# GpSimd's routed and output transfers wait for matmuls at chosen places instead of for copies of their row numbers

## The chip, the cores and the metric

The kernel runs on one core of a Trainium2 chip. The metric is the device time of one execution in microseconds (us), the median of three runs. TensorE (PE in the profile) multiplies matrices, VectorE (DVE), ScalarE (ACT) and GpSimd (POOL) work on rows, and SyncE (SP) issues most of the plain transfers. GpSimd issues the indirect ones, whose destination rows come from a column of row numbers in on-chip memory.

## The reference, cut to what matters

A long convolution of 8 sequences of 5056 steps and 128 channels is followed by a mixture of experts with 4 groups of 4 experts. Every token goes to the best expert of its best group.

```python
# x: [8, 5056, 128], h: [5056, 128]
L = 2 * S
y = np.fft.irfft(np.fft.rfft(x, n=L, axis=1) * np.fft.rfft(h, n=L, axis=0)[None], n=L, axis=1)[:, :S, :]
x = y.reshape(40448, 128)
g_logits = x @ w_group                       # 4 groups
g_idx, g_w = argmax, softmax weight of it
for g in range(4):
    e_logits = xg @ w_expert[g]              # 4 experts of the group
    e_idx, e_w = argmax, softmax weight of it
    for e in range(4):
        h = np.maximum(xg[mask_e] @ w1[g, e], 0.0)   # 128 -> 1024
        out[tok_idx] = g_w * e_w * (h @ w2[g, e])    # 1024 -> 128
```

## The kernel before, in words

The convolution is done as Fourier transforms written as matmuls, in three rounds r = 0, 1, 2 of at most three sequences. A round has a first stage (`stage1`, matmuls of L427 and L433, whose results ScalarE and VectorE copy and combine in L444 to L450) and then `groups`: a forward transform (L531), the multiplication by the transform of h on VectorE (L549), an addition (L583), an inverse transform (L599) and a copy `zs` on ScalarE (L612) that is stored to memory.

Beside the main list of each later round runs a `side` list with the tokens of the round before: the last inverse transform (L734 to L748, copied to `yT` in L755), transposes (L791) into rows `rw` (L792), the logits (L802 to L812), and the gate on VectorE (`gate_math`, L910 to L1003), which ends in `posf` (L1003): for each token the row of the array `srt` in which it is to lie, so that tokens of one expert lie together. Then `srt` receives the rows: for each 128 tokens one closure of `scatter` (L863) stands in the list `sends`. `send()` takes the next closure. It copies one column of `posf` to the integers `pos` (L867), on VectorE or on ScalarE as the caller asks, and lets GpSimd issue the indirect transfer of L868 out of `rw`. Calls of `send` stand at fixed places of the main list.

The experts are then worked off in blocks of 512 tokens, each in 8 steps. A step has three matmuls of the first layer (`mm1`, L1374 to L1376, into `px` or `aux`), the ReLU on ScalarE (L1379) and the rest of its split on VectorE (L1380), and three matmuls of the second layer (`mm2`, L1392 to L1394, into `pz` or `ptr`). ScalarE copies the result (`oT`, L1397), TensorE turns it (L1408), VectorE scales it (`orow`, L1412), and `scatter_out` lets GpSimd issue one indirect transfer to `out` for each 128 rows (L1445). In the blocks that have a fixed place in the program (`timed`) ScalarE first copies the column of row numbers, `ids` or `kept_ids`, to a tile `at` of which there are 8 (L1443). Some blocks of rows go out to memory and come back later as `take`. From about 1485 us the last blocks run, whose transfers use `sids` and no copy.

The order of every engine's instructions is that of the program; nothing reorders it. `run` writes the main list, and `weave` puts the side lists between its steps by weights. A transfer that GpSimd issues waits, before the change, for the engine that wrote its column of row numbers. Thus the place of the copy on ScalarE or VectorE sets when a transfer starts.

Of the kernel before, what the change touches and what calls it, by code (L numbers as in the profile page):

```python
# [232 lines left out]
class Kernel:  # L233
# [5 lines left out]
    def pools(self, ctx):  # L239
# [5 lines left out]
        self.turns, self.beside, self.sends, self.tick = 0, "", [], 0  # L245
# [136 lines left out]
    def stage1(self, r):  # L382
# [32 lines left out]
        def mm(k):  # L415
# [7 lines left out]
            for j in range(h * QB // 2, (h + 1) * QB // 2):  # L423
                if fold:
                    for b in range(2):
                        for c in range(2):
                            nc.tensor.matmul(  # L427
# [4 lines left out]
                else:  # L432
                    nc.tensor.matmul(  # L433
# [37 lines left out]
    def groups(self, r):  # L471
# [42 lines left out]
        def forward(p):  # L514
# [7 lines left out]
            for i, (to, of, w) in enumerate(steps):  # L522
                for b in range(2):
                    rows = slice(b * 64, b * 64 + 64)
                    for c in range(2):
# [5 lines left out]
                        nc.tensor.matmul(  # L531
                            px[c * 64:c * 64 + 64, b, to], lhsT=k, rhs=data[:, of],
                            start=begin, stop=i == len(steps) - 1 or p == 0 and i == 1, tile_position=(b * 64, c * 64),
                        )
            if r == 0:
# [21 lines left out]
        def product(p):  # L557
# [9 lines left out]
            self.send("a")  # L567
# [8 lines left out]
            if r == 2 and p % 2 == 0 and len(self.sends) > 12:  # L576
                self.send("a")
# [9 lines left out]
        def inverse(p):  # L587
# [7 lines left out]
            for part in range(2):  # L595
                wt, k = (cgs[p + LP], 320 - part * 64) if p > 0 else (first[0], part * 128)
                for c in range(n):
                    for h in (0, 64):
                        nc.tensor.matmul(  # L599
# [46 lines left out]
        def step(k):  # L646
# [4 lines left out]
            self.tick += 1  # L651
# [47 lines left out]
    def side(self, r):  # L699
# [39 lines left out]
        def rest(n):  # L739

            zt = zts.pop(n // 4)
            for u in range(nu):
                for q in (n // QB, n // QB + 1):
                    k = q % 2 * QB * RT
                    for c in (0, 64):
                        d = c * nu + u * HD
                        both = pys[q][c:c + 64, 0:QB * c1].rearrange("p (i u m) -> p i u m", i=QB, u=nu)[:, :, u]
                        nc.tensor.matmul(  # L748
# [4 lines left out]
            for q in (n // QB, n // QB + 1):  # L753
                k = QB * q % 8 * c1
                nc.scalar.copy(out=self.yT[:, k:k + QB * c1], in_=pys.pop(q)[:, 0:QB * c1])  # L755

        def lump(k):
            def f():
# [8 lines left out]
                rest(4 * k)  # L767

# [9 lines left out]
        def rows(i):  # L778
# [10 lines left out]
            for j in range(n):  # L789
                k = (4 * i + j) * GP  # L790
                nc.tensor.transpose(out=pt[:, j * D:(j + 1) * D], in_=self.yT[:, k:k + GP], identity=self.ident)  # L791
# [38 lines left out]
        for o in range(N2 // 8):  # L830
# [3 lines left out]
            if r < 2:  # L834
# [3 lines left out]
                at.append((t + 4.7, both(lm, lambda: rows(0)), False))  # L838
                at.append((t + 6.4, both(lt, lambda: rows(1)), False))
                at.append((t + 9.5, both(*more), False))  # L840
                at += [(t + 6.5 + 5.6 * k / (NMATH + REST), advance(ops), True) for k in range(NMATH + REST)]
                at.append((t + 12.15, lambda o=o, s=sends: self.sends.extend((8 * r + o, f, self.tick) for f in s), True))
            else:
# [4 lines left out]
                at.append((t + 3, both(lm, lambda: rows(0)), False))  # L848
                at.append((t + 4, both(lt, lambda: rows(1)), False))
                at.append((t + 5, both(*more), False))  # L850
                at += [(t + 4.02 + 3.3 * k / (NMATH + REST2), advance(ops), True) for k in range(NMATH + REST2)]
                at.append((t + 7.4, lambda o=o, s=sends: self.sends.extend((8 * r + o, f, self.tick) for f in s), True))
# [10 lines left out]
    def scatter(self, k, j, p, r, T):  # L863


        def f(copy):
# [920 lines left out]
```

## Time and profile before

| | before |
|---|---|
| median of 3 runs (lowest, highest) | 1764.83 us (1753.78, 1769.3) |
| the profiled execution, its span | 1761.84 us, 1760.3 us |
| mean granted clock of TensorE | 0.989 |
| TensorE busy | 1649.6 us, 94% |
| VectorE busy | 1317.5 us, 75% |
| ScalarE busy | 1118.5 us, 64% |
| GpSimd busy | 763.5 us, 43% |

The span is the profiled execution from its first to its last recorded instruction. Busy time counts an engine's own instructions, without register and semaphore work. Four stretches of the span bear on the change: rounds 1 and 2 with their side lists (192 to 700 us), the expert blocks beside which the last tokens are routed (700 to 1116 us), the expert blocks with output transfers at fixed places (1116 to 1485 us), and the last blocks (1485 to 1760 us). In the rows below, "idle" is an engine's time without work just ahead of an instruction, and the name behind the arrow is what ended it. "issue" means that the engine waited for nothing that the profile shows.

### The profile page before, as it was taken

What the parts mean: (1) busy time and instruction counts of PE and PEld (TensorE: products, weight loads), DVE (VectorE), ACT (ScalarE), POOL (GpSimd) and SP (SyncE); (2) the same over time, 40 slices, a digit from 0 to 9 for tenths busy, and PEclk for the clock granted to TensorE, in tenths of its full rate; (3) what the DMA queues carried; (4) which work ended last, traced back from release to release, by engine and by line L of the source; (5) the groups of instructions that cost most, each with busy time, mean ns of one, the idle gap of its engine ahead of it and who ended that gap; (6) DMA issues with size and microseconds to landing.
All of it is one profiled execution on the core that took longest, in us unless ns stands there. A gap on an engine that the chain in (4) does not pass through costs nothing. (4 is left out here: it accounts for less than half of the span.)

```text
span 1760.3 us, 47512 instructions
## 1 busy us (share of the span) xinstructions
PE 1649.6 (94%) x16576; PEld 1267.6 (72%) x16576; DVE 1317.5 (75%) x2969; ACT 1118.5 (64%) x2645; POOL 763.5 (43%) x730
## 2 busy tenths in 40 slices
PE   8998898988889898999999999999999999999998
PEld 7676745546755554777777777787777877888987
DVE  6554587864567677687787778888788888887888
ACT  5554444443444444677777777677777777776876
POOL 1451232333244445325455545345555555334545
PEclk9999999998999999999999999999999999999999
DMA  7797576766666787676666755476965687555667
GB/s 212 225 289 214 161 230 215 254 204 201 176 199 212 232 242 214 176 187 178 166 177 165 176 151 142 115 177 185 213 171 138 167 216 199 141 135 147 165 159 176
DMA packets 403939, 330.22 MB, mean 188 GB/s; under 512 B 167708, under 2 KB 347425, under 8 KB 403672
## 3 DMA queue, kind: packets, MB, share of 16 engines
q1 hardware_dynamic: 374808, 271.01, 56.9%
q0 software_dynamic: 20608, 41.79, 7.3%
q10 hardware_dynamic: 8256, 14.10, 2.8%
q8 instruction: 139, 2.28, 0.6%
q14 instruction: 128, 1.05, 0.2%
HBM read 208.00 MB, written 96.86 MB: 173 GB/s over the span
## 5 line engine op out<-in xcount | busy, mean ns | idle before, releaser
L868 POOL DMA_INDIRECT srt<-rw,pos x320 | 334.0, 1044 | 491.1 <-ACT pos L867 141.0
L1445 POOL DMA_INDIRECT out<-orow,at x176 | 190.8, 1084 | 237.1 <-ACT at L1443 122.9
L549 DVE TENSOR_TENSOR y<-pp,hg 128x768 f32<-128x768 f32 (+1 forms) x108 | 92.5, 857 | 93.9 <-ACT hg L539 33.4
L1445 POOL DMA_INDIRECT out<-orow,sids x92 | 96.2, 1045 | 114.8 <-DVE orow L1412 89.3
L599 PE MATMUL pp<-y,cg 64*64 64x384 f32 (+1 forms) x1504 | 132.0, 444 | 13.2 <-issue 6.5
L531 PE MATMUL pp<-st,cg 64*64 64x192 f32 (+1 forms) x1588 | 121.5, 404 | 4.0 <-issue 1.9
L755 ACT COPY yT<-py 128x474 f32<-128x474 f32 (+1 forms) x96 | 44.7, 513 | 116.8 <-PE py L748 88.5
L612 ACT COPY zs<-pp 128x768 f32<-128x768 f32 (+1 forms) x106 | 75.6, 714 | 64.5 <-PE pp L599 38.2
L445 DVE TENSOR_TENSOR st<-pp,odd 128x320 f32<-128x320 f32 x96 | 46.9, 489 | 91.4 <-ACT odd L444 87.4
L734 PE MATMUL py<-ig,zm 126*64 126x79 f32 x2048 | 92.3, 237 | 21.6 <-issue 18.8
L734 PEld LDWEIGHTS py<-ig,zm 126*64 126x64 f32 x2048 | 78.9, 137 | 43.1 <-issue 35.1
L599 PEld LDWEIGHTS pp<-y,cg 64*64 64x64 f32 x1504 | 62.4, 132 | 61.5 <-issue 40.2
L1380 DVE SCALAR_TENSOR_TENSOR h3l<-px,h3h 128x512 fp32r<-128x512 f32 (+1 forms) x111 | 74.4, 671 | 40.9 <-ACT h3h L1379 39.1
L1380 DVE SCALAR_TENSOR_TENSOR h0l<-px,h0h 128x512 fp32r<-128x512 f32 (+1 forms) x109 | 73.3, 672 | 37.2 <-ACT h0h L1379 26.5
L531 PEld LDWEIGHTS pp<-st,cg 64*64 64x64 f32 x1588 | 66.5, 133 | 43.5 <-issue 29.6
L1379 ACT ACTIVATE h0h<-px 128x512 fp32r<-128x512 f32 (+1 forms) x109 | 64.0, 587 | 50.8 <-PE px L1376 38.0
L1380 DVE SCALAR_TENSOR_TENSOR h2l<-px,h2h 128x512 fp32r<-128x512 f32 (+1 forms) x112 | 75.3, 672 | 23.8 <-ACT h2h L1379 15.3
L549 DVE TENSOR_TENSOR m<-pp,hg 128x768 f32<-128x768 f32 (+1 forms) x108 | 91.5, 847 | 0.0
L792 ACT COPY rw<-py 128x1024 uint16<-128x1024 uint16 (+1 forms) x88 | 81.1, 938 | 16.1 <-remote 6.8
L1379 ACT ACTIVATE h3h<-px 128x512 fp32r<-128x512 f32 (+1 forms) x111 | 65.3, 589 | 32.4 <-PE px L1376 20.9
L583 POOL TENSOR_TENSOR y<-y,m 128x512 f32<-128x512 f32 x40 | 50.9, 1277 | 77.3 <-DMA hd<-hg 43.0
L1380 DVE SCALAR_TENSOR_TENSOR h1l<-px,h1h 128x512 fp32r<-128x512 f32 (+1 forms) x111 | 74.4, 671 | 11.3 <-issue 7.7
(482 smaller groups left out, 5248.3 us busy)
## 6 DMA issues: line engine op xcount, KB each, us to landing
wr<-in_moe_w SPq DMA_DIRECT2D x373, 256.0 KB
zd<-zs SPq DMA_DIRECT2D x66, 384.0 KB
zm<-zd SPq DMA_DIRECT2D x64, 378.0 KB
cg<-in_c_g SPq DMA_DIRECT2D x106, 224.0 KB
zd<-zs SPq DMA_DIRECT2D x39, 256.0 KB
hg<-hd SPq DMA_DIRECT2D x68, 128.0 KB
xt<-in_x ACTq DMA_DIRECT2D x52, 160.0 KB
zm<-zd SPq DMA_DIRECT2D x32, 252.0 KB
```

What stands on the lines that cost most here:

```text
L445: nc.vector.tensor_tensor(out=all_st[:, 0:2 * HALF, d], in0=even, in1=odd, op=ALU.add)
L531: nc.tensor.matmul(px[c * 64:c * 64 + 64, b, to], lhsT=k, rhs=data[:, of], start=begin, stop=i == len(steps) - 1 or p == 0 and i == 1, til ...
L549: nc.vector.tensor_tensor(out=t[:, :, 0:w].rearrange("p t (r u d) -> p t r u d", r=2, u=nu), in0=taken(px, part).unsqueeze(1).broadcast_to ...
L583: (nc.gpsimd if r == 0 else nc.vector).tensor_tensor(out=y[:, :, 0:w], in0=y[:, :, 0:w], in1=m[:, :, 0:w], op=ALU.add)
L599: nc.tensor.matmul(pz[c][h:h + 64, 0:w], lhsT=wt[c * 64:c * 64 + 64, k + h:k + h + 64], rhs=y[c * 64:c * 64 + 64, part, 0:w], start=part = ...
L612: nc.scalar.copy(out=z[:, 0:n, 0:w], in_=pp[:, 0:n, 0:w])
L734: nc.tensor.matmul(pys[q][c:c + 64, col(n, u)], lhsT=zms[q][:, n % QB, k:k + 64], rhs=self.ig[:, 0:NH], start=n % QB == 0 and u == 0, stop ...
L792: nc.scalar.copy(out=od["rw"][i // 2][:, 4 * i % RH:4 * i % RH + n, 0:2 * D].rearrange("p j (h d) -> p j h d", h=2), in_=pt[:, 0:n * D].bi ...
L868: ins = self.nc.gpsimd.indirect_dma_start(out=self.srt, out_offset=bass.IndirectOffsetOnAxis(ap=k["pos"][0:p, j:j + 1], axis=0), in_=k["rw ...
L1379: nc.scalar.activation(out=hh, in_=p, func=AF.Relu)
L1380: nc.vector.scalar_tensor_tensor(out=hl, in0=p, scalar=0.0, in1=hh.bitcast(F32), op0=ALU.max, op1=ALU.subtract)
L1445: ins = self.nc.gpsimd.indirect_dma_start(out=self.a["out"], out_offset=bass.IndirectOffsetOnAxis(ap=ids, axis=0), in_=o, in_offset=None, ...
```

## The change

The copies of L867 and L1443 are gone. The gate's last multiplication writes the integers `pos` itself, and output transfers read `ids` or `kept_ids` itself. In their place the program keeps in `self.mark` the latest matmul of certain kinds, and a new function `behind` makes a transfer wait for the one that is in `mark` when the transfer is written into the program. Marks are set in the first stage, in the forward and inverse transforms, in the side lists' matmuls and transposes, and at the last matmul of each `mm1` and each `mm2`. The calls of `send` have partly other places: fewer in the first stage and in the transforms, new ones in the side lists (`beside`) while these run next to a round, and at every step of the first expert blocks.

```diff
@@ stage1, groups, side: marks @@
-                    nc.tensor.matmul(
+                    self.mark = nc.tensor.matmul(
                         whole[:, j * 256:j * 256 + N1], lhsT=views[i][:, j * 128:j * 128 + 128], rhs=self.f,
...
+                if i == 1 and p % 2 == 0:
+                    self.mark = last
...
-                        nc.tensor.matmul(
+                        last = nc.tensor.matmul(
                             px[c * 64:c * 64 + 64, b, to], lhsT=k, rhs=data[:, of],
...
+            if p % 2 == 1:
+                self.mark = last
...
@@ groups: places of send @@
-            self.send("a")
+            self.send()
             yield
             m = multiply(px, p, 1, "m", 2)
...
-            if r == 2 and p % 2 == 0 and len(self.sends) > 12:
-                self.send("a")
...
-                    if p == k:
-                        self.send("a")
...
-                    if r == 2 or i == 1:
-                        self.send("s")
+                    if i == 1 or len(self.sends) > 20:
+                        self.send()
@@ side @@
+        def beside():
+            if self.beside != "experts":
+                self.send()
...
-                at.append((t + 4.7, both(lm, lambda: rows(0)), False))
+                at.append((t + 4.7, both(lm, lambda: rows(0), beside), False))
@@ scatter, send, behind @@
-        def f(copy):
-            copy(out=k["pos"][:, j:j + 1], in_=k["posf"][:, j:j + 1])
+        def f():
             ins = self.nc.gpsimd.indirect_dma_start(
                 out=self.srt,
...
+            self.behind(ins)
...
-    def send(self, eng="v"):
-
-        if eng == "a":
-            eng = "s" if self.sends and self.sends[0][2] < self.tick else "v"
+    def send(self):
+
         if self.sends:
-            self.sends.pop(0)[1](self.nc.vector.tensor_copy if eng == "v" else self.nc.scalar.copy)
+            self.sends.pop(0)[1]()
+
+    def behind(self, ins):
+
+        if self.mark is not None:
+            info = mybir.DependencyInfo(mybir.DependencyClass.Sync, mybir.DependencyReason.DATA)
+            self.tc.add_manual_dep(ins.ins, self.mark.ins.name, info, reason="transfers are issued one by one")
@@ gate_math @@
-        posf = tl([], "posf", bufs=2)
+        posf = tl([], "posf")
...
-        nc.vector.tensor_tensor(out=posf, in0=posf, in1=sg, op=ALU.mult)
-        k["posf"] = posf
         k["pos"] = cx.tile([128, 15], I32, name="pos", bufs=3)[0:P, 0:T]
+        nc.vector.tensor_tensor(out=k["pos"], in0=posf, in1=sg, op=ALU.mult)
@@ mm1, mm2 @@
-            nc.tensor.matmul(o, lhsT=wh[:, k:k + 128], rhs=xl, start=False, stop=True)
+            self.mark = nc.tensor.matmul(o, lhsT=wh[:, k:k + 128], rhs=xl, start=False, stop=True)
...
-            nc.tensor.matmul(p, lhsT=wh[:, k:k + 128], rhs=hl, start=False, stop=f == 7)
+            self.mark = nc.tensor.matmul(p, lhsT=wh[:, k:k + 128], rhs=hl, start=False, stop=f == 7)
@@ scatter_out @@
-            if timed:
-                at = self.fx.tile([128, 1], I32, name="at", bufs=8)
-                self.nc.scalar.copy(out=at, in_=ids)
-                ids = at
...
+            if timed:
+                self.behind(ins)
@@ run @@
-                        if r > 0 and k % 2 == 1:
+                        if r > 0 and k % 4 == 1:
                             add(self.send)
...
-                    elif k < 8 * (NA - 2) and k % 8 not in (3, 4, 5, 6):
-                        add(lambda: self.send("s"))
+                    elif k < 8 * (NA - 2) and (k < 8 * (N0 - 2) or k % 8 not in (3, 4, 5, 6)):
+                        add(lambda: self.send())
```

The built programs show what this does to the order of the engines. TensorE's and SyncE's instructions stand in the same order as before. GpSimd has the same 552 transfers in the stretches of the change; 21 of those to `srt` stand at another place among those to `out`. In the rows below, a name with `_49` in brackets is a wait for that engine's semaphore, `DMASW` is one of GpSimd's own earlier transfers, and `DMAHW` a transfer of another queue.

On GpSimd, in an expert block of the third stretch, the transfers of two blocks and of one `take` stood like this before:

```order
L1445 DMA out<-orow,at 40448x128 [waits DMASW0_49,DVE_49,Activation_49]
L1445 DMA out<-orow,at 40448x128 [waits DMASW1_49,Activation_49]
...
L1445 DMA out<-orow,at 40448x128 [waits DMASW4_49,DVE_49,Activation_49]
L1445 DMA out<-orow,at 40448x128 [waits DMASW5_49,Activation_49]
...
L1445 DMA out<-take,at 40448x128 [waits DMAHW4_49,DMASW0_49,Activation_49]
L1445 DMA out<-take,at 40448x128 [waits DMASW1_49,Activation_49]
```

and stand so now:

```order
L1450 DMA out<-orow,ids 40448x128 [waits DMASW0_49,DVE_49,PE_49]
L1450 DMA out<-orow,ids 40448x128 [waits DMASW1_49,PE_49]
...
L1450 DMA out<-orow,ids 40448x128 [waits DMASW4_49,DVE_49,PE_49]
L1450 DMA out<-orow,ids 40448x128 [waits DMASW5_49,PE_49]
...
L1450 DMA out<-take,kept_ids 40448x128 [waits DMAHW4_49,DMASW0_49,PE_49]
L1450 DMA out<-take,kept_ids 40448x128 [waits DMASW1_49,PE_49]
```

The order is the same, the wait for ScalarE (Activation) has become one for TensorE (PE), and the source of the row numbers is the tile itself. Of all 552 transfers 509 waited for ScalarE before, and 534 wait for TensorE now; to that end 590 more matmuls raise a semaphore.

On ScalarE, at about the same place, between the ReLUs of L1379 (line L1388 now) and the splitting of weights (L1316, L1325 now), there stood before:

```order
L1379 ACTIVATE h2h<-aux 128x512 [waits PE_49]
L1316 CAST w2h<-wr_19652 128x512 [waits DMAHW1_49]
L1443 COPY at<-ids 128x1 [waits DMASW3_49]
L1379 ACTIVATE h3h<-px 128x512 [waits PE_49]
L1443 COPY at<-kept_ids 128x1 [waits DMASW4_49]
L1379 ACTIVATE h0h<-px 128x512 [waits PE_49]
L1316 CAST w1h<-wr_19654 128x512 [waits DMAHW2_49]
L1443 COPY at<-kept_ids 128x1 [waits DMASW5_49]
L1379 ACTIVATE h1h<-aux 128x512 [waits DVE_49,PE_49]
```

and there stands now:

```order
L1388 ACTIVATE h2h<-aux 128x512 [waits PE_49]
L1325 CAST w2h<-wr_19070 128x512 [waits DMAHW1_49]
L1388 ACTIVATE h3h<-px 128x512 [waits PE_49]
L1388 ACTIVATE h0h<-px 128x512 [waits PE_49]
L1325 CAST w1h<-wr_19072 128x512 [waits DMAHW2_49]
L1388 ACTIVATE h1h<-aux 128x512 [waits DVE_49,PE_49]
```

The copies between the ReLUs are gone, and with them ScalarE's waits for GpSimd's earlier transfers; the rest stands as it stood.

On GpSimd, in the first routed transfers of round 1, there stood before:

```order
L868 DMA srt<-rw,pos 331776x260 [waits DVE_49,Activation_49]
L868 DMA srt<-rw,pos 331776x260 [waits DVE_49] x3
...
L868 DMA srt<-rw,pos 331776x260 [waits DMASW1_49,DVE_49]
L868 DMA srt<-rw,pos 331776x260 [waits DMASW2_49,Activation_49]
```

and there stands now:

```order
L873 DMA srt<-rw,pos 331776x260 [waits DVE_49,PE_49,Activation_49]
L873 DMA srt<-rw,pos 331776x260 [waits PE_49] x3
...
L873 DMA srt<-rw,pos 331776x260 [waits DMASW1_49,PE_49]
L873 DMA srt<-rw,pos 331776x260 [waits DVE_49,DMASW2_49,PE_49,Activation_49]
```

Here each wait for the copy, on VectorE or ScalarE, has become one for a matmul, and the first transfer out of a set of rows waits for the gate and the rows themselves as well.

## Rows read from the trace of the kernel before

**Rows 1.** The page's head: the span.

```profile
span 1760.3 us, 47512 instructions
```

**Rows 2.** Windows: stretch, its length, busy us (instructions), PEclk, DMA share, GB/s.

```profile
core 0: us, PE busy (x) PEld busy (x) DVE busy (x) ACT busy (x) POOL busy (x), PEclk, DMA share, GB/s
...
192.00:700.00 508.00, 446.83 (x6763) 283.34 (x6754) 353.04 (x858) 230.77 (x630) 194.32 (x191) 0.97 0.69 211
700.00:1116.00 416.00, 406.30 (x2866) 320.92 (x2865) 322.35 (x749) 306.87 (x710) 199.22 (x187) 0.99 0.66 170
1116.00:1485.00 369.00, 357.73 (x1601) 285.81 (x1601) 302.09 (x631) 277.20 (x648) 193.09 (x181) 1.00 0.69 176
```

**Rows 3.** Waits of PE, 192 to 700: total us, times, longest.

```profile
PE py L734 <- issue: 16.6, 35, 1.3
...
PE pp L599 <- DVE m L549: 4.0, 5, 1.3
...
PE py L812 <- ACT lT L807: 1.2, 1, 1.2
```

**Rows 4.** Waits of PE, 700 to 1116.

```profile
PE pz L1394 <- DVE h3l L1380: 2.4, 3, 1.0
...
PE ptr L1392 <- ACT h3h L1379: 0.3, 1, 0.3
```

**Rows 5.** Waits of PE, 1116 to 1485.

```profile
PE ptr L1408 <- ACT oT L1397: 4.6, 3, 2.3
...
PE ptr L1394 <- DVE h2l L1380: 0.2, 1, 0.2
```

**Rows 6.** Lines of ACT: busy us, mean ns, idle before and its releaser.

```profile
L867 ACT CAST pos<-posf 128x1 int32<-128x1 f32 x268 | 49.2, 194 | 7.1 <-DVE posf L1003 7.1
...
L1443 ACT COPY at<-ids 128x1 int32<-128x1 int32 x176 | 33.5, 190 | 0.0
...
L1443 ACT COPY at<-kept_ids 128x1 int32<-128x1 int32 x56 | 11.0, 196 | 0.0
```

**Rows 7.** Lines of DVE: the copy of places.

```profile
L867 DVE CAST pos<-posf 128x1 int32<-128x1 f32 x52 | 6.9, 144 | 0.1
```

**Rows 8.** Timeline of ACT: start us, length us, instruction.

```profile
1320.39 0.20 ACT L1443 COPY at<-kept_ids 128x1 int32<-128x1 int32 x1
1320.48 0.61 ACT L1379 ACTIVATE h2h<-px 128x512 fp32r<-128x512 f32 x1
```

**Rows 9.** Lines of POOL: the transfers.

```profile
L868 POOL DMA_INDIRECT srt<-rw,pos x320 | 334.0, 1044 | 491.1 <-ACT pos L867 141.0 <-issue 80.6 <-ACT st L450 48.5
L1445 POOL DMA_INDIRECT out<-orow,at x176 | 190.8, 1084 | 237.1 <-ACT at L1443 122.9 <-ACT x L1324 61.0 <-issue 31.3
```

**Rows 10.** Timeline of PE, 1338.6 to 1343, idle time before in brackets.

```profile
1338.68 0.39 PE L1376 MATMUL px<-x0l,w1h 128*128 128x512 f32 x1
1338.91 0.39 PE L1392 MATMUL pz<-h1h,w3h 128*128 128x512 f32 x1
...
1340.04 0.39 PE L1376 MATMUL aux<-x1l,w0h 128*128 128x512 f32 x1
...
1341.40 0.39 PE L1376 MATMUL px<-x1l,w0h 128*128 128x512 f32 x1
1342.47 0.50 PE L1392 MATMUL pz<-h3h,w3h 128*128 128x512 f32 x1 [0.68 <-ACT h3h L1379]
```

**Rows 11.** Timeline of ACT, the ReLU on the first of these.

```profile
1341.82 0.60 ACT L1379 ACTIVATE h3h<-px 128x512 fp32r<-128x512 f32 x1 [2.88 <-PE px L1376]
```

**Rows 12.** Timeline of POOL, the transfers of the same moment.

```profile
1336.88 1.04 POOL L1445 DMA_INDIRECT out<-orow,at  x1 [0.30 <-issue]
1338.22 0.98 POOL L1445 DMA_INDIRECT out<-orow,at  x1 [0.30 <-issue]
1339.51 1.01 POOL L1445 DMA_INDIRECT out<-orow,at  x1 [0.30 <-issue]
```

**Rows 13.** Timeline of ACT: first and last of the 32 late starts.

```profile
505.50 0.55 ACT L755 COPY yT<-py 128x474 f32<-128x474 f32 x1 [3.20 <-remote]
...
1447.01 0.60 ACT L1379 ACTIVATE h0h<-aux 128x512 fp32r<-128x512 f32 x1 [1.71 <-PE aux L1376]
```

More of the change, by code (lines that the diff above doesn't have):

```diff
@@ L244, in pools @@
         self.pq = self.banks.enter_context(tc.tile_pool(name="pq", bufs=4, space=PSUM))
-        self.turns, self.beside, self.sends, self.tick = 0, "", [], 0
+        self.turns, self.beside, self.sends, self.mark = 0, "", [], None
     def share(self):
@@ L432, in mm @@
                 else:
-                    nc.tensor.matmul(
+                    self.mark = nc.tensor.matmul(
                         whole[:, j * 256:j * 256 + N1], lhsT=views[i][:, j * 128:j * 128 + 128], rhs=self.f,
@@ L598, in inverse @@
                     for h in (0, 64):
-                        nc.tensor.matmul(
+                        self.mark = nc.tensor.matmul(
                             pz[c][h:h + 64, 0:w], lhsT=wt[c * 64:c * 64 + 64, k + h:k + h + 64],
@@ L747, in rest @@
                         both = pys[q][c:c + 64, 0:QB * c1].rearrange("p (i u m) -> p i u m", i=QB, u=nu)[:, :, u]
-                        nc.tensor.matmul(
+                        self.mark = nc.tensor.matmul(
                             both, lhsT=zt[k:k + QB * RT, d:d + 64],
@@ L767, in f @@
                 rest(4 * k)
+                beside()
             return f
@@ L790, in rows @@
                 k = (4 * i + j) * GP
-                nc.tensor.transpose(out=pt[:, j * D:(j + 1) * D], in_=self.yT[:, k:k + GP], identity=self.ident)
+                self.mark = nc.tensor.transpose(
+                    out=pt[:, j * D:(j + 1) * D], in_=self.yT[:, k:k + GP], identity=self.ident
+                )
             nc.scalar.copy(
@@ L837, in side @@
                 at.append((t + 3, lump(2 * o + 1), False))
[L838 to L840 removed]
+                at.append((t + 4.7, both(lm, lambda: rows(0), beside), False))
+                at.append((t + 6.4, both(lt, lambda: rows(1), beside), False))
+                at.append((t + 9.5, both(*more, beside), False))
                 at += [(t + 6.5 + 5.6 * k / (NMATH + REST), advance(ops), True) for k in range(NMATH + REST)]
[L842 removed]
+                at.append((t + 12.15, lambda o=o, s=sends: self.sends.extend((8 * r + o, f) for f in s), True))
             else:
@@ L847, in side @@
                 at.append((t + 2, lump(2 * o + 1), False))
-                at.append((t + 3, both(lm, lambda: rows(0)), False))
-                at.append((t + 4, both(lt, lambda: rows(1)), False))
-                at.append((t + 5, both(*more), False))
+                at.append((t + 3, both(lm, lambda: rows(0), beside), False))
+                at.append((t + 4, both(lt, lambda: rows(1), beside), False))
+                at.append((t + 5, both(*more, beside), False))
                 at += [(t + 4.02 + 3.3 * k / (NMATH + REST2), advance(ops), True) for k in range(NMATH + REST2)]
-                at.append((t + 7.4, lambda o=o, s=sends: self.sends.extend((8 * r + o, f, self.tick) for f in s), True))
+                at.append((t + 7.4, lambda o=o, s=sends: self.sends.extend((8 * r + o, f) for f in s), True))
         at.sort(key=lambda x: x[0])
@@ L1535, in act @@
                         self.put()
-                        self.send("s")
+                        self.send()
                     elif prev:
```

2 lines of the change are left out of this document (removed).

## The prediction

> **What bounds the kernel now.** I read the span first, then the engines' busy time by stretch, then what ended TensorE's idle time, and last the two engines that the change touches. The profiled execution took 1761.84 us, with a span of 1760.3 us [rows 1], so 1.5 us lie around it. That is 3.0 us (0.2%) under the median of 1764.83 us. TensorE is busy for 94% of the span. The stretches show where it is not [rows 2]: of 508.0 us in rounds 1 and 2 (192 to 700 us) it is idle for 61.2, of 416.0 us in the first expert stretch (700 to 1116) for 9.7, of 369.0 us in the second (1116 to 1485) for 11.3. The 192 us before and the 275 us behind these hold almost nothing that the change touches. So the most that any edit to GpSimd's transfers could free is the part of these 82 us that a late result of ScalarE or VectorE ends.
>
> The waits of TensorE split them. From 192 to 700 us the largest group is "issue", in which TensorE waited for nothing that the profile shows: 16.6 us ahead of L734 alone [rows 3]. What a late ScalarE or VectorE result ended, in groups of 1 us or more, is 13 waits with 15.7 us, from the first row (m L549, 4.0 us) to the last (lT L807, 1.2 us). From 700 to 1116 us it is 7 waits with 6.2 us (first and last group in [rows 4]), from 1116 to 1485 us 12 waits with 13.1 us (first and last in [rows 5]). Together: 32 waits, 35.0 us; in the expert stretches alone 19.3 us.
>
> **What goes.** ScalarE loses 268 casts of L867 (194 ns each) and 176 + 56 copies of L1443 (190 and 196 ns), together 500 instructions with 93.7 us of busy time [rows 6]. VectorE loses 52 casts of 144 ns [rows 7], 7.5 us by count times mean. These are not to be taken off the span. ScalarE is busy for 277.20 of 369.0 and 306.87 of 416.0 us in the expert stretches [rows 2], so it has gaps for them. The copies of L1443 were never what ScalarE waited with: idle time ahead of them is 0.0, and ahead of L867 it is 7.1 us in all [rows 6].
>
> What a copy costs the chain is the slot that it takes ahead of an instruction whose input is there. The trace shows one: the copy of 0.20 us starts at 1320.39, and the ReLU queued behind it starts at 1320.48 [rows 8], 0.09 us later, because consecutive instructions overlap. A copy on the path thus costs 0.09 us, and the nearest upper bound is its whole length, 0.20 us. Each of the 32 waits can have had one such slot in the run of work before it. One each gives 32 x 0.09 = **2.9 us**. The lower bound is 0 (all 32 stand behind something else), the upper is two whole copies in each, 32 x 0.40 = 12.8 us. I take one slot each: where the run of ScalarE's work ahead of such a wait holds a copy at all, it is seldom more than one, and the chain of a wait goes back over more runs than the last.
>
> VectorE's 52 casts I cost at nothing. VectorE is idle for 66.9 us or more in every one of the three stretches [rows 2], and that gap hides them; without it they would be 7.5 us. The position is now written as an integer by the multiplication that wrote it as a float: the same columns, once, nothing. One buffer of posf for two, and the index tiles held until the transfer has read them, are nothing too: the rings have 8 index tiles, so a tile is due some 8 blocks later, while a transfer is issued within a few steps.
>
> **What is added.** Each of the 552 transfers now waits for a matmul, not a copy. GpSimd's rows say what they wait for today: 141.0 us of its idle time ahead of L868 ends with the cast of L867, 122.9 us ahead of L1445 with the copy of L1443 [rows 9]. A copy sat behind a ReLU that waits for the same matmuls, so the moment hardly moves: taking in the trace of before the end of the matmul that each transfer now awaits, issue comes 1 to 2 us earlier on average in the expert stretches. Behind a waiting transfer hardly anything but transfers is queued (of the memsets of L412 four, the last at 400.3 us, of some 0.5 us). Who waits for a transfer is the next writer of its source buffer, at the nearest 12.6 us after the moved issue in that same alignment, against one transfer's 1.0 us and some microseconds of landing. I cost this at nothing. The moved places in the rounds change the order of 21 routed transfers among output transfers and of none on TensorE; that is nothing as well.
>
> On TensorE 590 more matmuls carry a semaphore increment. The matmul behind one that already does shows no delay: L1376 starts at 1338.68, the next at 1338.91 [rows 10], 0.23 us as everywhere. My bound from the difference of the medians (227 against 226 ns over these matmuls) is 0.01 us each, for 534 waiting transfers 5.3 us at the very most; I take nothing, since the row shows none. The Trainium skill ("TensorE: Matmul & The Clock Gate", section "The cost: per-tile semaphore tail") says that increments of tiled matmuls are serialised at 26.3 ns each. By that figure 534 of them would be an estimated 14 us, a time of about 1773 us; no run here shows it for whole-width matmuls, and rows 10 speak against it.
>
> **The sum.** 1761.84 - 2.9 + 0 = **1759 us**, 0.3% under the median; by the bounds of this case 1749 to 1762 us, and 1764 with the 5.3 us of increments and no gain.
>
> **The rivals.** *A: late increments go with the bunching.* ScalarE sometimes sees a finished matmul late. The matmul of L1376 begun at 1338.68 lasts 0.39 us [rows 10], yet the ReLU on it starts at 1341.82, after 2.88 us of idleness [rows 11]; two later ones (1340.04 and 1341.40) had been started by then, and TensorE stood still until 1342.47 [rows 10]. Meanwhile GpSimd issued transfers at 1336.88, 1338.22 and 1339.51, 1.3 us apart [rows 12]. From 480 to 1485 us 424 ScalarE instructions wait for a matmul, and 32 start more than 0.4 us late, from 505.50 to 1447.01 (first and last in [rows 13]). Of them 28 fall among the 159 beside a transfer that follows another within 1.45 us, 4 among the other 265. If pacing by matmuls ended this, the 19.3 us of the expert stretches and about 1 us of slots in the rounds would go: 1741 us (-1.3%). For it: the share of 28 in 32. Against it: one mark stands in each step of six matmuls, and steps are 1.36 us apart (1338.68, 1340.04, 1341.40 [rows 10]), the pace of the transfers today.
>
> *B: the trains grow, and late increments with them (slower).* By the same alignment, 134 of 178 transfers from 1116 to 1485 us would follow their predecessor within 1.42 us, against 92 today, and third or later ones in a train would be 72 against 24. A late start there costs 13.1 / 16 = 0.8 us (16 of the 32 lie in this stretch). In proportion to followers 16 become 23, in all 6 us more: 1765 us, no change. In proportion to third ones 48, 32 more, 26 us: 1785 us (+1.1%). It decides from about 29 further late starts on, which bring 1759 past 1782. Against it: transfers alone may not cause late starts, and 131 of 159 beside close followers started in time.
>
> *C: the increments cost* the 5.3 us: 1764 us. *D: the copies were hidden throughout,* and the change does nothing to the time: 1762 us.
>
> **How the numbers follow.** Forecast 0.45, A 0.2, B 0.2 (half of it beyond +1%), C 0.05, D 0.1. About 1% of 1764.83, 17.6 us, is what a measurement of this kernel can tell from no change, as its three runs lie 0.9% apart. Faster than 1747.2 is A: 0.2. Slower than 1782.5 is half of B: 0.1. The rest is 0.7. The range leaves out most of A's and of B's far halves, 2 in 10 together: 1744 to 1774 us. The likeliest case's own range is 1749 to 1764.
>
> **What would show it.** ScalarE's busy time falls by about 94 us to some 1025, and its row for L1379 keeps its duration. TensorE's idle time in 1116 to 1485 us stays within 2 us of 11.3, and the idle time ahead of L1445 is ended by TensorE lines. A is right if ScalarE's gaps above 0.4 us behind finished matmuls fall from 32 to under ten and TensorE's ScalarE- and VectorE-ended waits with them; B if they rise past 60 and stand within trains of transfers 1.36 us apart. I would be wrong from the ground if the rounds' 61.2 us of idleness moved by 10 us either way: nothing in my sum touches their "issue" part. Another sign against me is a new wait of a buffer's writer for a transfer.

## The result and the profile after

The changed kernel took 1720.65 us (median of 6 runs, 1715.1 to 1721.78), the kernel before beside it 1765.39 us (6 runs). The ratio is 0.9735, interval 0.9708 to 0.9763: 2.65% faster, where no change was forecast and 1744 to 1774 us was the range. The profiled execution took 1721.78 us.

TensorE has 16576 instructions in both traces, in the same order but for 98 places, so each matmul can be laid beside itself. Those that started at 200.0, 720.2, 1116.1 and 1485.2 us now start at 197.9, 680.9, 1076.7 and 1443.3 us. Of the 40 us of the profiled executions 2 are won before the rounds, **37 in the rounds**, 0 and 2.5 in the two expert stretches; the last blocks lose 2. These are the windows of the kernel before between those matmuls (stretch, its length, busy us and instructions of PE, PEld, DVE, ACT, POOL, granted clock, DMA share, GB/s):

```profile
200.00:720.20 520.20, 460.92 (x6727) 293.79 (x6728) 366.92 (x901) 239.86 (x653) 197.61 (x194) 0.97 0.69 209
720.20:1116.10 395.90, 386.73 (x2793) 306.18 (x2792) 306.43 (x698) 294.01 (x681) 190.88 (x179) 1.00 0.66 169
1116.10:1485.20 369.10, 357.83 (x1602) 285.88 (x1601) 302.09 (x631) 277.30 (x648) 193.09 (x181) 1.00 0.69 176
```

and those of the changed kernel:

```profile
197.90:680.90 483.00, 434.73 (x6740) 283.12 (x6730) 361.21 (x858) 230.63 (x506) 196.90 (x194) 0.98 0.74 226
680.90:1076.70 395.80, 387.83 (x2792) 307.69 (x2791) 306.49 (x694) 282.58 (x506) 186.88 (x180) 0.99 0.66 169
1076.70:1443.30 366.60, 358.55 (x1602) 288.83 (x1601) 302.75 (x631) 262.71 (x470) 188.17 (x181) 0.99 0.69 177
```

TensorE's busy time in the rounds fell by 26 us for the same matmuls. The mean length of one hardly moved (238 and 235 ns in the rows below); where matmuls start singly, they overlap less and together fill more time. The clock counts too: in places it was granted at 0.5, which is 1.2 GHz, and summed over windows of 2 us the time that this took from full speed was 16.7 us in the rounds before and 10.3 now. Laid beside each other by line, the time up to the next start shrank by 18.2 us ahead of L734 (line 733 now), 11.3 us ahead of L599 (601) and 4.5 us ahead of L748 (747). These are the rows of L734 in the rounds before and now (busy us, mean ns, idle time ahead and what ended it):

```profile
L734 PE MATMUL py<-ig,zm 126*64 126x79 f32 x1152 | 55.2, 238 | 19.3 <-issue 16.6 <-ACT rw L792 2.5
L733 PE MATMUL py<-ig,zm 126*64 126x79 f32 x1152 | 48.4, 235 | 7.9 <-ACT rw L798 4.9 <-issue 2.8
```

The waits of TensorE from 198 to 681 us after (total us, times, longest) begin so; the "issue" row that led [rows 3] with 16.6 us has come down to 2.8 (all "issue" rows of TensorE together, in the rounds: 39.1 us before, 19.5 now):

```profile
PE pp L601 <- DVE m L553: 9.4, 11, 2.3
PE pp L427 <- issue: 7.0, 15, 1.3
PE py L733 <- ACT rw L798: 4.9, 4, 2.5
...
PE py L733 <- issue: 2.8, 6, 1.3
```

What those "issue" waits were is seen when the timelines of GpSimd and TensorE are put side by side. This is GpSimd in the kernel before (start, length, instruction, idle time before it):

```profile
257.14 1.44 POOL L868 DMA_INDIRECT srt<-rw,pos  x1 [0.81 <-DVE pos L867]
258.88 0.97 POOL L868 DMA_INDIRECT srt<-rw,pos  x1 [0.30 <-ACT pos L867]
260.16 0.97 POOL L868 DMA_INDIRECT srt<-rw,pos  x1 [0.30 <-issue]
261.44 0.98 POOL L868 DMA_INDIRECT srt<-rw,pos  x1 [0.30 <-issue]
262.73 0.98 POOL L868 DMA_INDIRECT srt<-rw,pos  x1 [0.30 <-issue]
```

and this TensorE beside it:

```profile
259.72 0.97 PE L734 MATMUL py<-ig,zm 126*64 126x79 f32 x21
260.94 0.30 PE L734 MATMUL py<-ig,zm 126*64 126x79 f32 x2 [0.25 <-issue]
261.66 0.37 PE L734 MATMUL py<-ig,zm 126*64 126x79 f32 x3 [0.42 <-issue]
262.39 0.36 PE L734 MATMUL py<-ig,zm 126*64 126x79 f32 x4 [0.36 <-issue]
263.11 0.30 PE L734 MATMUL py<-ig,zm 126*64 126x79 f32 x2 [0.36 <-issue]
```

21 matmuls go through in 0.97 us; from the third transfer of the train on (260.16 us) only two to four each 0.72 us. The same matmuls after the change, where GpSimd issued at 249.78, 251.23, 252.51, 255.01 and 256.74:

```profile
253.30 0.36 PE L733 MATMUL py<-ig,zm 126*64 126x79 f32 x4
254.01 1.18 PE L733 MATMUL py<-ig,zm 126*64 126x79 f32 x27 [0.35 <-issue]
```

I call **followers** the transfers that start within 0.5 us of the end of the one before, and **thirds** those that are third or later in such a train. In the rounds thirds fell from 56 to 21, in the two expert stretches they went from 66 to 54 and from 91 to 100. What ends GpSimd's idle time ahead of an output transfer is now TensorE's lines ([rows 9] has the copies there). Ahead of the routed ones "issue" and a line of VectorE come first, TensorE third:

```profile
L873 POOL DMA_INDIRECT srt<-rw,pos x320 | 331.8, 1037 | 442.9 <-issue 53.5 <-DVE st L446 49.2 <-PE py L747 44.8
L1450 POOL DMA_INDIRECT out<-orow,ids x176 | 184.5, 1048 | 252.4 <-PE ptr L1403 69.0 <-PE pz L1403 68.9 <-PE px L1385 40.2
```

### The profile page after: what moved, and what is told of

The parts are those of the page before. It is cut to its first block, busy times and chain, and to the rows that moved or that the text cites. A ratio compares the mean times of both kernels' runs of the same rounds, so it can differ in the third digit from the quotient of the medians.

```text
span 1720.1 us, 46979 instructions
## 1 busy us (share of the span) xinstructions
PE 1627.1 (95%) x16576; PEld 1259.0 (73%) x16576; DVE 1311.6 (76%) x2917; ACT 1084.3 (63%) x2145; POOL 753.7 (44%) x730
## 5 line engine op out<-in xcount | busy, mean ns | idle before, releaser
L1450 POOL DMA_INDIRECT out<-orow,ids x176 | 184.5, 1048 | 252.4 <-PE ptr L1403 69.0
L601 PE MATMUL pp<-y,cg 64*64 64x384 f32 (+1 forms) x1504 | 125.8, 449 | 14.6 <-DVE m L553 8.3
L1388 ACT ACTIVATE h0h<-px 128x512 fp32r<-128x512 f32 (+1 forms) x109 | 64.0, 587 | 55.6 <-PE px L1385 39.1
L733 PEld LDWEIGHTS py<-ig,zm 126*64 126x64 f32 x2048 | 76.6, 139 | 29.7 <-issue 18.0
L733 PE MATMUL py<-ig,zm 126*64 126x79 f32 x2048 | 86.9, 237 | 11.4 <-issue 5.5
L1389 DVE SCALAR_TENSOR_TENSOR h2l<-px,h2h 128x512 fp32r<-128x512 f32 (+1 forms) x112 | 75.1, 671 | 26.5 <-ACT h2h L1388 21.2
L1388 ACT ACTIVATE h3h<-px 128x512 fp32r<-128x512 f32 (+1 forms) x111 | 65.4, 589 | 33.2 <-PE px L1385 14.7
L1388 ACT ACTIVATE h1h<-px 128x512 fp32r<-128x512 f32 (+1 forms) x111 | 65.3, 588 | 29.8 <-PE px L1385 13.2
```

The costliest lines, as they stand in the source:

```text
L601: self.mark = nc.tensor.matmul(pz[c][h:h + 64, 0:w], lhsT=wt[c * 64:c * 64 + 64, k + h:k + h + 64], rhs=y[c * 64:c * 64 + 64, part, 0:w], ...
L733: nc.tensor.matmul(pys[q][c:c + 64, col(n, u)], lhsT=zms[q][:, n % QB, k:k + 64], rhs=self.ig[:, 0:NH], start=n % QB == 0 and u == 0, stop ...
L1388: nc.scalar.activation(out=hh, in_=p, func=AF.Relu)
L1389: nc.vector.scalar_tensor_tensor(out=hl, in0=p, scalar=0.0, in1=hh.bitcast(F32), op0=ALU.max, op1=ALU.subtract)
L1450: ins = self.nc.gpsimd.indirect_dma_start(out=self.a["out"], out_offset=bass.IndirectOffsetOnAxis(ap=ids, axis=0), in_=o, in_offset=None, ...
```

## The experiments

TRAINS is the theory that transfers of GpSimd that follow each other at once stall the other engines, COPIES the rival that the 500 removed copies gave the time back. Ratios are to the kernel before, run on the same chip in turn; that kernel's own time differs between the occasions, and with it what there is to gain.

**Copies, waits and places apart.** Four kernels with the kernel before at 1763.48 us.

```diff
# e1: the changed kernel, no waits for marks
-        if self.mark is not None:
+        if False:
# e2: the changed kernel, a copy beside each transfer again
+            spare = self.cx.tile([128, 1], I32, name="spare", bufs=2)
+            self.nc.scalar.copy(out=spare[0:p], in_=k["pos"][0:p, j:j + 1])
# e4: the changed kernel, calls of send as before, for instance
-                        if r > 0 and k % 4 == 1:
+                        if r > 0 and k % 2 == 1:
# e5: the kernel before (with copies), calls of send as changed
```

> The changed kernel without the waits for marked matmuls: a transfer waits only for its data. Two theories. TRAINS: the gain comes from transfers that no longer follow each other at once. In rounds 1 and 2 the third or later transfers of a train (each begun within 0.5 us of the end of the one before) fell from 56 to 21, and the time between the same matmuls fell by 37 us there and nowhere else. Without marks the trains grow to the length of a set of rows, so the stalls come back: 1760 us or more, over 100 third or later transfers in the rounds. COPIES: the gain comes from the 500 copies that ScalarE and VectorE no longer make. They are gone here too: about 1721 us.

> The changed kernel with a copy of one column on ScalarE put back beside each of the 552 transfers, to a spare tile that nothing reads; the waits for marks stay. TRAINS: nothing but the slots of the copies, some 0 to 5 us: 1721 to 1726 us, third or later transfers in the rounds still about 21. COPIES: the gain is lost, about 1760 us.

> The waits for marks and no copies, but the transfers sent from the places of the kernel before. TRAINS: between the two kernels, by how many third or later transfers are left in the rounds: 21 give 1721 us, 56 give 1760 us, so about 1.1 us for each above 21. COPIES: about 1721 us.

> The kernel before, with its copies and its waits for them, but the transfers sent from the new places. TRAINS: by the count of third or later transfers in the rounds on the same scale (56 give 1760 us, 21 give 1721 us); if the places alone thin the trains, close to 1725 us. COPIES: about 1760 us, since all copies are there.

| | median us | ratio (interval) | rounds, us | thirds in rounds, experts |
|---|---|---|---|---|
| e1, no marks | 2068.78 | 1.1754 (1.1711 to 1.1797) | 626 | 152, 145, 110 |
| e2, copies back | 1721.26 | 0.9761 (0.9741 to 0.9781) | 483 | 22, 50, 104 |
| e4, old places | 1718.7 | 0.9752 (0.9729 to 0.9775) | 481 | 20, 54, 101 |
| e5, new places, copies | 1760.01 | 0.9972 (0.9947 to 0.9996) | 509 | 50, 68, 101 |

COPIES falls twice: with all 552 of them back the gain stays (e2), and with all of them gone but no marks the kernel takes 305 us more than before (e1). The places alone give 0.3% (e5), the waits give all of the gain, with copies (e2) or at the old places (e4). That the places might thin the trains, as I allowed for e5, hardly came: 56 thirds became 50. Removing the copies without pacing was the dangerous half of the change: the copies had held the transfers apart. In e1 (windows as above, the rounds and the first expert stretch) TensorE is idle for 100 us in each, and busy for some 60 us more than before, at a granted clock of 0.86 and 0.87:

```profile
205.20:831.40 626.20, 526.13 (x6737) 317.69 (x6730) 361.74 (x858) 230.54 (x506) 188.86 (x189) 0.86 0.57 173
831.40:1379.70 548.30, 446.10 (x2792) 330.32 (x2792) 305.78 (x695) 280.44 (x507) 183.60 (x184) 0.87 0.46 123
```

and its waits of 831 to 1380 us begin with ReLUs of ScalarE, for which TensorE waited up to 9.2 us at a time:

```profile
PE pz L1401 <- ACT h3h L1388: 26.2, 3, 9.2
PE ptr L1401 <- ACT h3h L1388: 22.3, 3, 8.9
PE py L747 <- issue: 18.2, 43, 1.4
```

**The stall by itself.** A kernel of its own, nothing of the reference in it. Each short matmul stands as two records in its trace.

```python
self.small({})                                   # 480 matmuls of 79 columns, no transfer
for n in (0, 1, 2, 3, 4, 6, 12):
    self.small({80: [self.routed] * n})          # n transfers behind matmul 80
self.small({40 + 30 * k: [self.routed] for k in range(12)})   # one each 30 matmuls
...
```

> A kernel of its own that computes nothing of the reference: TensorE runs stretches of 480 short matmuls (79 columns), and at one place of a stretch GpSimd issues a train of 0, 1, 2, 3, 4, 6 or 12 transfers of 128 rows, or 12 spaced by 30 matmuls, or 11 by 40; then trains of 12 with rows of 16 bytes, with 16 rows, by plain transfers of SyncE, and by plain ones of GpSimd; at last stretches of 96 long matmuls (512 columns) with no train, a train of 12, and 12 one each 6 matmuls. TRAINS: a stretch with 0, 1 or 2 transfers takes the same time, from 3 on it grows by roughly 0.7 us for each further transfer, so 12 add 6 to 10 us; spaced transfers add less than 2 us; the long matmuls lose less than the short ones. COPIES or a wait in the large kernel: every stretch with the same matmuls takes the same time within 1 us. Open: whether the rows' bytes or the issuing does it; if the bytes, the trains of 16-byte rows and of 16 rows add nothing, if the issuing, they add as much.

> The same stretches with four times the memory that GpSimd's transfers have for their lists (16384 for 4096 bytes). If a full list is what stalls the engines, trains of 12 add nothing or start to add later than at the third transfer; if the issuing itself does, the stretches are those of the run with 4096 bytes within 1 us.

| stretch of 480 short matmuls with | us |
|---|---|
| 0, 1 transfers | 32.8, 32.8 |
| 2, 3, 4, 6 in a train | 33.9, 35.2, 38.2, 40.9 |
| 12 in a train | 49.8 |
| 12 in a train, rows of 16 bytes; 16 rows each | 49.7; 49.1 |
| 12, one each 30 matmuls; 11, one each 40 | 33.5; 32.9 |
| 12 plain transfers by GpSimd; by SyncE | 32.8; 32.8 |

Each follower costs 1.1 us or more, the second transfer already, and twelve cost 17 us: more, and sooner, than I had expected. Neither the bytes nor the rows matter, nor the memory for the lists (the second kernel: 49.9 us for 12). Plain transfers by GpSimd at some 0.53 us from each other stall nothing. It is the indirect issue. A part of the cost of long trains is the clock. These are windows (as above) during the train of 12 (257.49 to 272.5 us), just behind it, and later:

```profile
257.50:272.50 15.00, 7.55 (x87) 4.68 (x82) 0.00 (x0) 0.00 (x0) 11.65 (x12) 0.69 0.15 49
275.00:280.00 5.00, 5.00 (x81) 5.00 (x80) 0.00 (x0) 0.29 (x2) 0.00 (x0) 0.50 0.01 3
282.00:287.00 5.00, 5.00 (x153) 5.00 (x151) 0.00 (x0) 0.53 (x2) 0.00 (x0) 1.00 0.02 3
```

TensorE was busy for half of the train, and behind it ran at a granted clock of 0.50 (1.2 GHz) for a while: 81 records in 5 us against 153, some 2.4 us lost there. ScalarE copies a result after each 40 matmuls; its timeline about the same train ("remote" is a release that the profile can't place):

```profile
254.45 0.27 ACT L67 COPY y<-p 128x128 f32<-128x128 f32 x1 [2.47 <-PE p L62]
257.19 0.27 ACT L67 COPY y<-p 128x128 f32<-128x128 f32 x1 [2.47 <-PE p L62]
274.75 0.27 ACT L67 COPY y<-p 128x128 f32<-128x128 f32 x1 [17.30 <-remote]
278.92 0.27 ACT L67 COPY y<-p 128x128 f32<-128x128 f32 x1 [3.89 <-PE p L62]
```

The copy at 274.75 started 11.0 us after the end of its last matmul, and 2.2 us after the train: what TensorE reports reaches ScalarE late. The 96 long matmuls took 21.8 us with and without the train, but the copies behind them came later and later during the train, up to 5.1 us, and caught up 2 us behind it. With one transfer each six long matmuls (1.36 us) copies came at most 1.2 us late. So short matmuls suffer at once, long ones only when a late result is needed.

**Spacing without marks, and trains with them.** The kernel before took 1788.16 us here.

```diff
# e6: the kernel before, behind each routed and timed output transfer
+        self.nc.gpsimd.memset(self.idle, 0.0)      # 128 x 384, 0.44 us
# e3: the changed kernel, every third call of send releases three
+        self.calls = getattr(self, "calls", 0) + 1
+        for _ in range(3 if self.calls % 3 == 0 else 0):
```

> The kernel before with its copies, its waits and its places, and one memset of 128 x 384 elements on GpSimd behind each of the 552 transfers, so that two transfers start at least some 1.7 us apart and not 1.28. TRAINS: the gain comes without any mark: 1725 us, between 1715 and 1740. COPIES, or the wait for matmuls as such: 1763 us or more, since GpSimd only has more work.

> The changed kernel, but up to the last routed transfer (about 1080 us) every third call of send releases three transfers at once, all behind one mark. No copy, the same waits. TRAINS: third or later transfers in the rounds rise from 21 to about 60, so the time rises to about 1760 us. COPIES, or the wait for matmuls as such: 1721 us.

With the pause the kernel before, with its copies and waits, took 1695.5 us, ratio 0.947 (0.9414 to 0.9527), twice the gain of the change and more than I had expected, though GpSimd has 244.5 us more to do. The changed kernel was not run beside it, and the kernel before was 23 us slower here. The stretches say where the gain lies: the rounds took 484.5 us, no less than with the marks (483.0), but the expert stretches 386.1 and 352.8, where the marks left 395.8 and 366.6. The threes took 1775.58 us, ratio 0.9919 (0.9892 to 0.9946), with 73 thirds in the rounds, which took 517.0 us: marks and no copies, and the gain is two thirds gone.

```profile
L886 POOL MEMSET idle<- 128x384 uint16 x552 | 244.5, 443 | 0.4
```

**Which spacing, and where.** The spacing kernel has trains of 12 with memsets of w columns between them, then 12 transfers that each wait for a matmul so many matmuls further on.

```python
...
for w in (0, 16, 64, 128, 256, 384, 768):
    self.small({80: [lambda q: self.routed(q), lambda q, w=w: self.pause(w)] * 12})
for k in (20, 21, 22, 24, 27):
    self.small({40 + k * i: [self.routed] for i in range(12)})
...
```

> The kernel of short matmuls again: trains of 12 transfers with a memset of 0, 16, 64, 128, 256, 384 or 768 columns behind each, then 12 transfers that each wait for a matmul 20, 21, 22, 24 or 27 matmuls after the one before (1.37 to 1.85 us), then long matmuls with no train, a train of 12, one with memsets of 384 columns, and 12 one each 6 matmuls (1.36 us). TRAINS: without memset a stretch grows by 17 us, and the growth falls as the spacing rises from 1.28 us and is under 2 us from 1.57 us on. If any instruction between breaks the train, already 16 columns bring the growth to nothing. With long matmuls the ReLU-like copies of ScalarE start up to 5 us late behind a train of 12 and under 1 us late with the memsets.

> The changed kernel with the memset of 128 x 384 elements on GpSimd behind each of the 552 transfers, so that no two of them start closer than some 1.57 us. TRAINS: the 21 + 54 + 100 third or later transfers that the change left go too, so the time falls to that of the kernel before with the memset or a little under it (500 copies fewer): a ratio of 0.945 to the kernel before. If marks and pause did different things, their gains would add up: a ratio of 0.92.

> The same without the waits for marked matmuls: the kernel that took 2069 us, with the memset behind each transfer. Transfers are issued as soon as their data are there, up to 15 in a row, but 1.57 us apart. TRAINS: what counts is the spacing alone, so the ratio is again about 0.945 and the 300 us are gone. If a long row of transfers costs something of its own even when spaced: above 0.97.

> The kernel before with a much shorter memset of 128 x 32 elements (some 0.12 us) behind each transfer, so that the spacing stays near the 1.28 us of trains. If the spacing counts, most of the gain is lost: ratio 0.98 to 1.0. If any other instruction between two transfers breaks the train, the gain stays: ratio 0.947.

On this occasion the kernel before took 1654.16 us, 6 to 8% less than beside the others, and all three kernels were level with it: 1.003, 1.0025 and 1.0017, in the order above. The spacing kernel shows what was different: all its stretches behind the first took 32.8 us, with a train of 12 at 1.27 us too. Trains stalled nothing there. These runs tell nothing of the spacing, but they led to the next: the changed kernel itself where trains stall nothing.

> The spacing stretches again. Where trains stall: without memset a stretch of short matmuls grows from 32.8 us by some 17 us; the growth falls as the spacing rises from 1.28 us and is under 2 us at 1.57 us (384 columns) and with waits 24 matmuls apart (1.64 us). If any instruction between two transfers ended the stall, 16 columns would do. Where trains do not stall: 32.8 us throughout, as in the last call.

> The changed kernel beside the kernel before. Where trains stall: ratio 0.975. Where they do not: TRAINS says that nothing is left to gain, ratio 0.995 to 1.005; if the marks or the copies gave something of their own, it stays below 0.99 here too.

> The changed kernel with the memset of 384 columns behind each transfer. Where trains stall: ratio 0.945, all of the kernel before's stall gone. Where they do not: 1.00, as in the last call.

> The same without the waits for marks. Where trains stall: 0.945 if the spacing alone counts, above 0.97 if long rows of spaced transfers still cost something. Where they do not: 1.00.

It came out so again: 32.8 us in all stretches behind the first, the kernel before 1654.42 us, and the changed kernel **1.0017 (0.9998 to 1.0036)**; with the pause 1.0022, with the pause alone 1.0047. So without the stall the change gives nothing at all. The pause without marks was thus never measured where trains stall. The changed kernel's trace has 59 thirds in the rounds here, no fewer than the kernel before where trains stall (56), and the rounds take 445.3 us all the same:

```profile
197.90:643.20 445.30, 411.48 (x6737) 271.55 (x6730) 360.00 (x858) 229.92 (x505) 199.97 (x194) 0.98 0.80 245
```

Of TensorE's "issue" waits in the rounds only these two are left, 2.2 us, and none ahead of L733:

```profile
PE pp L601 <- issue: 1.3, 1, 1.3
PE pp L427 <- issue: 0.9, 1, 0.9
```

> The spacing stretches a third time. Where trains stall (the kernel before takes 1760 us or more beside it): a stretch of short matmuls grows from 32.8 us by some 17 us without memset, less with each step of spacing above 1.28 us, and by under 2 us from 1.57 us (384 columns) or 1.64 us (24 matmuls) on. Where they do not (1655 us beside it): 32.8 us throughout.

A third run of the spacing kernel (the kernel before 1765.91 us beside it) met the stall:

| 12 transfers with | start to start, us | added to 32.8 us |
|---|---|---|
| no memset; 16 columns; 64 | 1.27; 1.28; 1.29 | 16.7; 16.4; 15.7 |
| 128; 256; 384 | 1.35; 1.46; 1.57 | 15.0; 13.4; 9.0 |
| 768 columns | 1.89 | 0.4 |
| a wait 20 matmuls on (1.37 us unstalled) | 1.28 to 2.16, mostly 1.68 to 1.74 | 3.9 |
| 24 on (1.64 us); 27 on (1.85 us) | 1.73 to 1.80; 1.73 to 2.31 | 1.3; 0.5 |

Another instruction between two transfers is no help; the spacing is. 1.57 us, which I had expected to be enough, leaves 9.0 us of the 16.7 in a train of 12. With long matmuls it was enough: no copy behind them came over 0.1 us late. And the last rows show what a mark does that a pause does not. GpSimd's timeline with waits 20 matmuls apart:

```profile
390.58 0.97 POOL L35 DMA_INDIRECT srt<-rows,idx  x1 [7.94 <-PE p L66]
392.27 0.98 POOL L35 DMA_INDIRECT srt<-rows,idx  x1 [0.72 <-PE p L66]
394.00 0.98 POOL L35 DMA_INDIRECT srt<-rows,idx  x1 [0.75 <-PE p L66]
395.69 0.97 POOL L35 DMA_INDIRECT srt<-rows,idx  x1 [0.70 <-PE p L66]
```

20 short matmuls take 1.37 us unstalled, yet the transfers are 1.7 us apart (mostly 1.37 in the first run, where nothing stalled): the stalled matmuls come later, and with them the next transfer. A wait for a short matmul brakes the train that stalls it.

**The best of both.** The changed kernel with 768 columns behind each routed transfer and 384 behind each output transfer.

```diff
+            self.pause(768)      # in scatter
+                self.pause(384)  # in scatter_out, if timed
```

> The changed kernel with a memset of 768 columns behind each routed transfer (spacing 1.88 us) and of 384 behind each output transfer (1.57 us). Where trains stall: the rounds come down from 484 us to 450 or 460, so the ratio to the kernel before is 0.93, under the 0.947 of the kernel before with 384 columns; if it stays at 0.947, the rest in the rounds is not from transfers. Where trains do not stall: 1.00.

1677.02 us, the kernel before 1787.33 us beside it: ratio **0.9375** (0.9332 to 0.9418), below both kernels; e6, on another occasion, lies 18 us higher, and its interval just touches this one. The rounds take 469 us and the expert stretches 389 and 354, the latter two what the changed kernel takes where nothing stalls (389 and 352). Of the 24 us left in the rounds the runs don't show the cause; "issue" waits of TensorE are 9.4 us there, against 2.2 where nothing stalls, and the pauses' own work on GpSimd was not tried with 768 columns where nothing stalls. My expectation of 450 to 460 was too low.

```profile
193.90:663.10 469.20, 423.11 (x6738) 278.90 (x6731) 378.12 (x858) 230.13 (x506) 344.32 (x381) 0.96 0.75 232
663.10:1052.00 388.90, 384.30 (x2792) 304.99 (x2791) 323.97 (x696) 282.24 (x507) 297.66 (x353) 1.00 0.64 171
1052.00:1406.30 354.30, 351.30 (x1602) 288.23 (x1601) 308.95 (x633) 266.37 (x470) 266.90 (x365) 1.00 0.71 185
```

## Why the prediction was wrong

**The copies: right as far as the runs can tell, and beside the point.** The slots were put at 2.9 us. With all copies back e2 is 0.6 us slower than the changed kernel by the medians, 0.26% (4.6 us) by the ratios, whose intervals overlap. The sign named for the copies did not come: ScalarE's busy time fell by 34 us (1118.5 to 1084.3) and not by 94, since a copy overlaps what follows it [rows 8].

**The step that failed is the reading of "issue".** The prediction took the 16.6 us ahead of L734 [rows 3] as time that nothing in the change touches, because no instruction of another engine stood behind it, and so looked for a gain only among the 35.0 us that ScalarE and VectorE ended. The term for the rounds was thereby put at nothing but slots, and measured 37 us. Most of these "issue" waits were the stall: of the matmuls of L734 in the rounds that started more than 0.35 us behind the one before (34), none stood beside a first transfer of a train (152 matmuls), 4 of 106 beside a second, 11 of 71 beside a third, 7 of 36 beside a fourth, 3 of 11 beside a later one; 9 of 748 elsewhere. And where trains stall nothing, "issue" is down to 2.2 us. The prediction had named the sign itself, the rounds' idleness moving by 10 us either way: between the same matmuls it fell from 59.3 to 48.3 us. Putting the timelines of GpSimd and TensorE side by side at the largest "issue" row would have shown it. I did so only for ScalarE's late starts [rows 10 to 12].

**Rival A had the trains, but not the stall of the matmuls themselves, and the wrong stretch.** Late increments do go with trains: counted over both kernels, also for instructions that wait for more than TensorE, ScalarE's starts more than 0.4 us late fell from 31 (56.0 us) to 22 (26.5 us) in the rounds, but only from 39 (51.4 us) to 28 (35.4 us) in the expert stretches; "under ten", A's own sign, was not met. A was priced by the expert stretches alone, 19.3 us, and the rounds were given 1 us of slots; there the term was 37.

**The objection to A held where it was made.** "The pace of the transfers today": between 1116 and 1485 us the marks of successive transfers stand a step of 1.36 us apart, thirds rose from 91 to 100, and the stretch gained 2.5 us of 369. It was carried over to the rounds without looking: there the stall itself moves the marks, as in the small kernel, and thirds fell to 21 (59 where nothing stalls).

**Rival B was real, but for another change.** Longer trains cost far more than the 26 us that it named: e1 has 305. In the second expert stretch the marks kept them from growing much: B expected 134 transfers within 1.42 us of their predecessor, and the trace after has 102, against 92. The 24 that B took for third or later ones in a train are by the trace the fourth or later; third or later within 1.42 us were 44, and are 48 now.

**Rival C falls as the outcome, not as a small term.** Where nothing stalls, the whole change with its 590 further increments moved the time by +0.17% (-0.02 to +0.36), 3 us, at most 6; the 5.3 us of C lie within that, and a small gain from the copies could hide a part. The estimate of 14 us, worked out from the 26.3 ns that the Trainium skill ("TensorE: Matmul & The Clock Gate", section "The cost: per-tile semaphore tail") gives for the increments of tiled matmuls, is not met here: this run does not agree with carrying that figure over to a stream of matmuls.

## What to carry to other kernels

Idle time that "nothing in the profile" explains is a place to lay all engines' timelines side by side, GpSimd's first: several gaps of equal length in a burst of short matmuls stood beside another engine's work here. Keep indirect transfers of GpSimd apart (1.9 us here), by a wait for a matmul in a stretch of short ones or by a piece of work behind each, and test the spacing itself by adding such a piece before rewriting who waits for whom. A copy that costs nothing may still be what holds two transfers apart, so taking it out needs something in its place.

## What the runs showed of the hardware

- A train of indirect transfers 1.28 us apart stalls short matmuls (1.1 us for the second transfer, 17 us for twelve, with a granted clock of 0.5 behind the long ones) and delays TensorE's reports to other engines, by 11.0 us in the train of 12, 12.6 us with 16 columns between. Rows of 16 bytes, 16 rows and a four times larger list memory changed little (49.7, 49.1 and 49.9 us for 49.8); plain transfers 0.53 us apart did nothing. Why the indirect issue does this stays open.
- The stall is not there always. The same kernel before took 1763 to 1788 us on some occasions and 1654 us on others, and the spacing kernel ran with the stall (707.9 us) and without (609.6 us). The runs don't show what decides it. The chip's number on record does not: the same number stands beside an occasion with the stall (e3, e6) and one without (the first three kernels with pauses). A gain from spacing is only worth what the stall costs on the day.
